# Splitting the hidden-dimension matrix anew in row blocks 0 to 2 of an FNet + GEGLU kernel, and fetching parked sums later

## The chip, the cores and the metric

One core of one Trainium2 chip runs the whole program. The metric is device time in microseconds (us) for one execution. "The profile" is one profiled execution of the kernel before. Its engines are PE (matrix multiply), DVE (vector), ACT (scalar), POOL (GpSimd) and SP (which here only issues transfers).

## What is computed

Four layers alternate on x of 2048 rows by 512 columns, in fp32. Layers 0 and 2 mix tokens by a discrete Fourier transform, layers 1 and 3 are a gated feed-forward block:

```python
a = x @ dft_hid_re.T ; b = x @ dft_hid_im.T          # along the 512 columns
y = dft_seq_re @ a - dft_seq_im @ b                  # along the 2048 rows
x = x + y(layernorm(x))
x = x + (gelu(z @ w_gate) * (z @ w_up)) @ w_down     # z = layernorm(x)
```

## The kernel before, in words

**Precision by three products.** Each fp32 operand is split in two parts: ACT copies a 128x512 tile rounded to fp32r (`hi`, L122), DVE subtracts it from the source (`lo`, L124). `mm3` (L160 to L164) then issues three matmuls: hi by hi (L162), hi or lo by the other's lo or hi (L163, L164). So each tile that PE uses costs one ACT and one DVE instruction first, and each 128x512 tile is 256 KB in a transfer.

**The mixing layers.** `mix` takes the output rows in four row blocks of 512 (b = 0 to 3). For a block the products with the sequence matrices (`ws`) come first, in a Strassen-like form that shares sums of tiles: stage `S2` (`s2(b)`, L820) runs three chains T2, T1 and T3 over k = 0 to 7, staggered; stage `S4` two more. Between and behind them stand the products with the hidden matrices (`wh`, eight tiles (m, c)), in `hid_groups`. In layer 0 the order of stages (`plan`, L400) is FORE, which runs the first products of all four blocks, and then for each block S2, EARLY hid, S4, MID hid, LATE hid. For S2, `make_s2` (L343) forms from tiles of `ws` the sums s1 (L153), s3 and s2 (L150) on DVE, and each is then split.

**Parked sums.** FORE produces for blocks 1 to 3 four 128x512 tiles each (two sums and two "sum" tiles) which POOL writes to DRAM (`put_away`, L247, names `m` and `m_sum`). `fetched` (L252) has SP load them back: at the very head of `s2(b)` (L827 to L829), before any product of that stage. The two `m` tiles are used when chain T2 of the block ends (`based`, L758), the two `m_sum` tiles by the EARLY hid products.

**The hidden matrix.** In layer 0, block 0, each `wh` tile is loaded raw (one 256 KB load), split, used, and both parts are written to DRAM by POOL (`make_hid_first`, L380, with `kept`, L275, whose store is L281). All later blocks, and layer 2, load the two finished parts (two 256 KB loads) and split nothing (`make_hid`, L387).

**What sets the order.** `items` lists all streamed weight tiles. `load_next` (L288) has SP load them some items ahead, `split_next` splits them, `take` hands them to PE. Chores of other layers stand in block 0 too: the split of three down-projection weights, stored by POOL as `wc` (L281, L1010). Results leave through `x_add` (L202), also on POOL. Every engine runs its instructions in program order, and the order itself is made by a scheduler that simulates the program with a few numbers on the machine (`machine_as_traced`, L1396), one of them `DMA_PACKET_NS`. SP's and POOL's transfers are thus each one fixed row of instructions, and a transfer that may not start yet holds up all behind it on that engine.

Of the kernel before, what the change touches and what calls it, by code (L numbers as in the profile page):

```python
# [9 lines left out]
F32 = mybir.dt.float32  # L10
# [7 lines left out]
ND = D // P  # L18
# [25 lines left out]
NEAR_PAIR = 8  # L44
LEAD_PAIR = 4
WHD_AT = 6
GAPS = 1, 2, 1
LEAD = 3
NK = NS // 2
# [1 line left out]
SP_DELAY_NS = 3000  # L51
DEPTH = 1
DMA_BYTES_PER_NS = 21.5
DMA_PACKET_NS = 37


@with_exitstack
def fnet_geglu(ctx: ExitStack, tc: tile.TileContext, x_in, ws, wh, whc, wgu, wdc, out):
# [58 lines left out]
    def f32(ap):  # L117
        return ap.bitcast(F32)
# [133 lines left out]
    def fetched(key):  # L252
        t = sb.get()
        nc.sync.dma_start(t, away.pop(key))
        return t


    whs = {(m, c): dram.tile([P, 1024], F32, name=f"wh{m}_{c}") for m in range(2) for c in range(ND)}
# [13 lines left out]
    def halves(t):  # L272
        return t[:, :512], t[:, 512:]

    def kept(place, parts, by_name=False):  # L275
        for n, t in enumerate(parts):
            to, t = halves(place)[n], f32(t)
            if by_name:
                to = place.rearrange("p (h m c) -> p h m c", h=2, m=2)[:, :, n]
                t = t.rearrange("p (h c) -> p h c", h=2)  # L280
            nc.gpsimd.dma_start(to, t)  # L281


    items, needs, outside = [], {}, set()
# [41 lines left out]
    def plain(v):  # L326
        p = split_slot(v)
        sb.put(v)
        return p

    s1s, s2s, s3s, cs, held = {}, {}, {}, {}, {}
# [4 lines left out]
    def make_a11(k):  # L336

        def run(v):
            held[k] = v
            return split_slot(v)  # L340
        return run

    def make_s2(k, keep):  # L343
        def run(a21, a22, *a11):
            a11 = a11[0] if a11 else held.pop(k)
            s1 = a22
            if keep:
                held["A22", k], s1 = a22, sb.get()
            plus(s1, a21, a22)
            minus(a21, a11, a21)  # L350
            minus(a11, s1, a11)
            s1s[k], s2s[k], s3s[k] = s1, a11, a21
            return split_slot(a11)
        return run
# [4 lines left out]
    def make_s1(k):  # L359
        return lambda: plain(s1s.pop(k))  # L360

    def make_s3(k):
        return lambda: plain(s3s.pop(k))
# [9 lines left out]
    def product_parts(m, c):  # L373

        t = cs.pop((m, c))
        p = split_minus(t) if m else split_slot(t)
        sb.put(t)
        return p

    def make_hid_first(m, c):  # L380
        def run(v):
            w = plain(v)
            kept(whs[m, c], w)
            return product_parts(m, c), w
        return run

# [3 lines left out]
    def skewed(n):  # L390

        skew = SKEW[n - 2]
        return [(i, k - i * skew) for k in range(NK + (n - 1) * skew) for i in range(n) if 0 <= k - i * skew < NK]
# [6 lines left out]
    def plan(layer):  # L400

        fore, steps = FORE[layer], []
        if layer == 0:
            steps += [(None, "FORE")]
        else:
            steps += [(b, "A11") for b in range(fore)] + [(b, "A12") for b in range(fore)]
        for b in range(NB):
            if b >= fore:
                steps += [(b, "A11"), (b, "A12")]
            if b in PAIRED[layer] or b - 1 in PAIRED[layer]:  # L410
                steps += [(b, "S2"), (b, "S4")] + [(b, "PAIR")] * (b - 1 in PAIRED[layer])
            else:
                steps += [(b, "S2"), (b, EARLY_HID), (b, "S4"), (b, MID_HID), (b, LATE_HID)]
        return steps
# [15 lines left out]
    def mix_items(layer):  # L430
        def raw(make, *tiles):
            items.append((F32, tiles, make, None))

        for b, what in plan(layer):
            if what == "FORE":
                for j in range(NS):
                    for c in range(FORE[layer]):
                        raw(plain, ws[c * 2 * NS + j])
                continue
            tiles = [[ws[(b * 2 + m) * NS + k] for k in range(NS)] for m in range(2)]  # L440
            (a11, a12), (a21, a22) = ((r[:NK], r[NK:]) for r in tiles)
            hold = b >= FORE[layer]
            if what == "A11":
                for k in range(NK):
                    raw(make_a11(k) if hold else plain, a11[k])
            elif what == "A12":
                for k in range(NK):
                    raw(plain, a12[k])
            elif what == "S2":
                for i, k in skewed(3):  # L450
                    if i == 0:
                        raw(make_s2(k, b in KEEP22[layer]), a21[k], a22[k], *(() if hold else (a11[k],)))
                    else:
                        raw(make_s1(k) if i == 1 else make_s3(k))
            elif what == "S4":
                for i, k in skewed(2):
                    if i == 0:
                        raw(make_s4(k), a12[k])
                    elif b in KEEP22[layer]:
                        raw(make_a22(k))  # L460
                    else:
                        raw(plain, a22[k])
            elif what == "PAIR":
                for name, k in PAIR_ORDER:
                    items.append((F32R, (piece_of(whd, k, name),), whole, NEAR_PAIR))
            else:
                for m, c in what:
                    if layer == 0 and b == 0:
                        items.append((F32, (wh[m * ND + c],), make_hid_first(m, c), (m, c)))
                    else:  # L470
                        items.append((F32R, halves(whs[m, c]), make_hid(m, c), (m, c)))

# [235 lines left out]
    def mix(layer):  # L708
        hid, sums, chores, hid_left = {}, {}, [], [0]
# [110 lines left out]
        def s2(b):  # L820
            last, fore = b == NB - 1, b < FORE[layer]
            if b == 0:
                lend("z")
                lend("x")
            if fore:
                chains[b] = [ps8.get() for _ in range(2)]
                if b:  # L827
                    sums[b] = [fetched((layer, b, c)) for c in range(2)]
                    cs.update({(0, c): fetched((layer, b, c, "sum")) for c in range(2)})  # L829
            chain, one, three = chains.pop(b), [ps8.get() for _ in range(2)], [ps8.get() for _ in range(2)]  # L830
            sides[b] = one, three
            if last:
                queue.extend([run for fetch in later.pop("fetches") for run in (None, None, None, None, fetch)])
            for i, k in skewed(3):
                if i == 0:
                    six(chain, "T2", k, fore and k == 0, k == NK - 1)
                elif i == 1:
                    six(one, "T1", k, k == 0, k == NK - 1, "T12" if last else None)
                else:
                    six(three, "T3", k, k == 0, k == NK - 1)  # L840
                if k < NK - 1:
                    continue
                if i == 0:
                    us[b] = [based(b, c, p) for c, p in enumerate(chain)]
                    ps8.put(*chain)
                    if fore:
                        sb.put(*sums.pop(b))
                for c in range(2):
                    if i == 1:
                        v = cs[1, 2 + c] = sb.get()  # L850
                        plus(v, us[b][c], one[c])
                    elif i == 2:
                        plus(cs[1, 2 + c], cs[1, 2 + c], three[c])
# [203 lines left out]
    def geglu(w, layer):  # L1057
# [50 lines left out]
        def up(n):  # L1108
            if layer == 1 and w == 0:
# [4 lines left out]
                if n % 2 == 0 and n // 2 + 1 in down_making:  # L1114
                    queue.extend(down_making.pop(n // 2 + 1)[1])
            if layer == w == 1 and 0 <= n - WHD_AT < ND and PAIRED[2]:
                load, runs = weight_steps(n - WHD_AT, whc, whd)
                load()
# [186 lines left out]
        if before_mix:  # L1305
            lend("x")
            lend("z")
            for k in (*range(NT, NK), *range(NT)):
                queue.extend([lambda k=k: second_rows(layer + 1, k), *[None] * GAPS[0]])
            for k in range(NK):  # L1310
                queue.extend([lambda k=k: combine(k), *[None] * GAPS[1]])
            for k in range(NK):
                queue.extend([lambda k=k: combine_late(k), *[None] * GAPS[2]])

# [63 lines left out]
    sums = [run for k in range(NK) for run in (lambda k=k: combine(k), lambda k=k: combine_late(k))]  # L1378
# [17 lines left out]
def machine_as_traced():  # L1396
# [7 lines left out]
    spec.DMA_BUS_BYTES_PER_NS_PER_ENGINE = DMA_BYTES_PER_NS  # L1404
    spec.DMA_MIN_TRANSFER_TIME = DMA_PACKET_NS
    depth = {mybir.EngineType.DVE: DEPTH, mybir.EngineType.Activation: DEPTH}
# [53 lines left out]
```

## Time and profile before

| what | value |
|---|---|
| median of 3 timed runs | 1598.64 us (1596.57, 1598.84, 1598.64) |
| the profiled execution itself | 1597.56 us |
| its span, first to last instruction | 1595.8 us |
| busy: PE, DVE, ACT, POOL | 1585.2, 1236.1, 857.9, 235.9 us |
| granted TensorE clock | 1.000 |

Busy time of PE hides small waits, so PE's rate is the better gauge: how many matmuls start in a stretch of time. In the tables of stretches below, each engine has its busy time and, in brackets, the number of its instructions. "Issue to landing" of a transfer is the time from its issue instruction to its last byte's signal. Queue q1 is SP's, q0 is POOL's.

### The profile page before, as it was taken

To read this page: it belongs to the slowest core of one execution; us is meant where nothing else is said; L and a number is where in the kernel's file an instruction comes from. 1 tells how busy PE (TensorE), PEld (TensorE's weight loads), DVE (VectorE), ACT (ScalarE), POOL (GpSimd) and SP (SyncE) were. 2 spreads that over 40 slices of the span, in tenths; PEclk is the share of its full clock that TensorE was granted. 3 is DMA by queue.
4 is the path that set the end of the run, shared out by engine and by line. 5 is a ranking of instruction groups with operands and counts; after the bars stand their busy time and mean duration, and the time that the engine had idled before them with its cause. 6 is when DMAs were issued, how large, how long until landed. Compare 5 with 4: busy or idle time off the path is not lost.

```text
span 1595.8 us, 23078 instructions
## 1 busy us (share of the span) xinstructions
PE 1585.2 (99%) x7026; PEld 1312.0 (82%) x7026; DVE 1236.1 (77%) x2148; ACT 857.9 (54%) x1680; POOL 235.9 (15%) x410
## 2 busy tenths in 40 slices
PE   9999999999999999999999999999999999999998
PEld 7888788888888888888888888888888888888887
DVE  8999979689789695666869987788985458754475
ACT  7864454545766652756777434446446435433361
POOL 2212300112545201330032000001002000000000
PEclk9999999999999999999999999999999999999999
DMA  9949987787999899996876687768998966896452
GB/s 360 326 167 321 358 279 235 235 292 259 338 341 325 283 346 305 305 323 199 310 231 234 241 269 247 245 236 239 254 375 226 293 204 229 302 280 203 137 190 56
DMA packets 251804, 422.86 MB, mean 265 GB/s; under 512 B 28864, under 2 KB 82112, under 8 KB 250656
## 3 DMA queue, kind: packets, MB, share of 16 engines
q1 hardware_dynamic: 227024, 338.26, 66.0%
q0 software_dynamic: 23840, 82.73, 14.2%
q8 instruction: 56, 0.92, 0.2%
q10 hardware_dynamic: 816, 0.39, 0.1%
q14 instruction: 68, 0.56, 0.1%
HBM read 339.74 MB, written 81.53 MB: 264 GB/s over the span
## 4 chain that ended last, share of the span: by engine, by line
PE 93%; DVE 3%; DMA 2%; issue 1%; ACT 1%; SPq 0%; POOL 0%; DVEq 0%; ACTq 0%; POOLq 0%
PE p L163 31%; PE p L164 31%; PE p L162 31%; DVE s L124 2%; DMA s<-ws 1%; DVE s L150 1%; ACT s L122 0%; DMA xwide<-ws 0%; DVE s L153 0%; DMA wc<-s 0%; DMA xwide<-wh 0%; SPq L298 0%; ACT s L553 0%; DVE st L512 0%; DVE xwide L150 0%
## 5 line engine op out<-in xcount | busy, mean ns | idle before, releaser
L163 PE MATMUL p<-s,s 128*128 128x512 f32 (+1 forms) x2334 | 902.2, 388 | 0.1
L164 PE MATMUL p<-s,s 128*128 128x512 f32 (+1 forms) x2334 | 891.5, 388 | 0.0
L162 PE MATMUL p<-s,s 128*128 128x512 f32 (+1 forms) x2334 | 874.1, 388 | 3.0 <-ACT s L122 2.7
L122 ACT ACTIVATE s<-s 128x512 fp32r<-128x512 f32 (+1 forms) x839 | 471.7, 608 | 341.6 <-DVE s L150 115.1
L124 DVE TENSOR_TENSOR s<-s,s 128x512 fp32r<-128x512 f32 (+1 forms) x839 | 526.5, 661 | 64.9 <-ACT s L122 55.6
L162 PEld LDWEIGHTS p<-s,s 128*128 128x128 f32 x2334 | 438.0, 188 | 95.6 <-ACT s L122 5.1
L163 PEld LDWEIGHTS p<-s,s 128*128 128x128 f32 x2334 | 438.2, 188 | 90.7 <-DVE s L124 0.9
L164 PEld LDWEIGHTS p<-s,s 128*128 128x128 f32 x2334 | 438.2, 188 | 89.8
L153 DVE TENSOR_TENSOR s<-s,p 128x512 f32<-128x512 f32 x291 | 195.4, 682 | 205.1 <-PE p L164 112.2
L150 DVE TENSOR_TENSOR s<-s,s 128x512 f32<-128x512 f32 (+1 forms) x411 | 247.0, 616 | 8.4 <-PE p L163 3.0
L157 ACT ACTIVATE s<-p 128x512 f32<-128x512 f32 x246 | 143.6, 593 | 150.0 <-PE p L164 140.5
L1054 ACT ACTIVATE s<-s 128x512 f32<-128x512 f32 x112 | 70.1, 629 | 119.0 <-DVE s L153 117.0
L281 POOL DMA_DIRECT2D wb<-s x84 | 46.7, 564 | 120.2 <-ACT s L122 89.9
L1068 DVE TENSOR_TENSOR s<-s,s 128x512 f32<-128x512 f32 x84 | 57.8, 688 | 1.8
L153 DVE TENSOR_TENSOR s<-s,s 128x512 f32<-128x512 f32 (+1 forms) x73 | 42.9, 591 | 8.9 <-DMA s<-ws 5.9
L122 ACT ACTIVATE s<-xwide 128x512 fp32r<-128x512 f32 (+1 forms) x61 | 36.8, 616 | 23.8 <-DVE xwide L150 5.1
L553 ACT ACTIVATE s<-s,shift,rstd 128x512 f32<-128x512 f32 x58 | 46.2, 806 | 4.2 <-DVE shift L517 4.1
L526 POOL TENSOR_SCALAR rstd<-rstd 128x1 f32<-128x1 f32 x48 | 15.4, 320 | 222.4 <-ACT junk L525 221.9
L243 POOL DMA_DIRECT2D out<-wide x8 | 5.2, 656 | 271.6 <-DVE wide L153 181.0
L124 DVE TENSOR_TENSOR s<-xwide,s 128x512 fp32r<-128x512 f32 (+1 forms) x61 | 40.5, 674 | 2.3 <-ACT s L122 2.2
L243 POOL DMA_DIRECT2D x<-wide x12 | 7.9, 661 | 219.1 <-DVE wide L153 146.5
L523 ACT ACTIVATE junk<-s 128x512 f32<-128x512 f32 x43 | 26.8, 624 | 22.4 <-DMA s<-x 22.2
(107 smaller groups left out, 520.7 us busy)
## 6 DMA issues: line engine op xcount, KB each, us to landing
s<-ws SPq DMA_DIRECT2D x367, 256.0 KB, 5.1
s<-wb SPq DMA_DIRECT2D x294, 256.0 KB, 5.3
s<-wc SPq DMA_DIRECT2D x196, 256.0 KB, 4.7
wb<-s POOLq DMA_DIRECT2D x98, 256.0 KB, 4.8
s<-wh SPq DMA_DIRECT2D x85, 256.0 KB, 5.2
s<-x SPq DMA_DIRECT2D x55, 256.0 KB, 4.6
xwide<-ws SPq DMA_DIRECT2D x49, 256.0 KB, 4.0
wc<-s POOLq DMA_DIRECT2D x49, 256.0 KB, 6.1
```

The source lines that it names most:

```text
L122: nc.scalar.activation(hi, src, AF.Copy)
L124: nc.vector.tensor_tensor(lo, src, f32(hi), op=ALU.subtract)
L150: nc.vector.tensor_tensor(out, a, b, op=ALU.subtract)
L153: nc.vector.tensor_tensor(out, a, b, op=ALU.add)
L157: nc.scalar.activation(v, src, AF.Copy)
L162: nc.tensor.matmul(ps, ah, bh, start=start, stop=False, skip_group_check=True)
L163: nc.tensor.matmul(ps, ah, bl, start=False, stop=False, skip_group_check=True)
L164: nc.tensor.matmul(ps, al, bh, start=False, stop=stop, skip_group_check=True)
L281: nc.gpsimd.dma_start(to, t)
L553: nc.scalar.activation(z, x, AF.Identity, bias=shift, scale=rstd)
L1054: nc.scalar.activation(t, g, AF.Gelu_apprx_tanh)
L1068: nc.vector.tensor_tensor(t, t, v, op=ALU.mult)
```

## The change

Three things change, all for layer 0, and nothing else in what is computed.

- Blocks 0, 1 and 2 (`KEEP_AT = 2`) load `wh` raw and split it anew. Only block 2 stores the parts. Block 3 and layer 2 load the stored parts as before.
- In blocks 1 to 3 the two `m` loads stand at k = 4 of chain T2 and the two `m_sum` loads at k = 7 (`BACK_AT = 4, 7`). In layer 2 all four stand at k = 0.
- `DMA_PACKET_NS`, a number of the scheduler's machine, is 39 instead of 37.

```diff
+BACK_AT = 4, 7
+KEEP_AT = 2
...
-DMA_PACKET_NS = 37
+DMA_PACKET_NS = 39
...
-    def make_hid_first(m, c):
+    def make_hid_first(m, c, keep):
         def run(v):
             w = plain(v)
-            kept(whs[m, c], w)
+            if keep:
+                kept(whs[m, c], w)
             return product_parts(m, c), w
         return run
...
-                    if layer == 0 and b == 0:
-                        items.append((F32, (wh[m * ND + c],), make_hid_first(m, c), (m, c)))
+                    if layer == 0 and b <= KEEP_AT:
+                        items.append((F32, (wh[m * ND + c],), make_hid_first(m, c, b == KEEP_AT), (m, c)))
...
             if fore:
                 chains[b] = [ps8.get() for _ in range(2)]
-                if b:
-                    sums[b] = [fetched((layer, b, c)) for c in range(2)]
-                    cs.update({(0, c): fetched((layer, b, c, "sum")) for c in range(2)})
...
             for i, k in skewed(3):
+                if b and fore and i == 0 and k == (0 if layer else BACK_AT[0]):
+                    sums[b] = [fetched((layer, b, c)) for c in range(2)]
+                if b and fore and i == 0 and k == (0 if layer else BACK_AT[1]):
+                    cs.update({(0, c): fetched((layer, b, c, "sum")) for c in range(2)})
```

In the changed kernel's rows below, line numbers are two to four higher: L300 is the old L298 (a load of the weight stream), L256 the old L254 (a fetch), L283 the old L281 (a store of parts), L155 and L152 the old L153 and L150.

**SP, head of block 1's S2.** Before, behind block 0's loads of `x`: two `ws` tiles, three parked tiles, then the third tile of the first pair of sums (s_2231), and so on.

```order
L190 DMA s_2199<-x 128x512
L298 DMA s_2233<-ws 128x512
L298 DMA s_2229<-ws 128x512
L254 DMA s_2278<-m_1_0_sum 128x512
L254 DMA s_2274<-m_1_0_1369 128x512
L254 DMA s_2276<-m_1_1_1375 128x512
L298 DMA s_2231<-ws 128x512
L298 DMA s_2308<-ws 128x512
L298 DMA s_2306<-ws 128x512
```

The same place in the changed kernel; s_2215 is the tile that corresponds to s_2231.

```order
L192 DMA s_2183<-x 128x512
L300 DMA s_2213<-ws 128x512
L300 DMA s_2282<-ws 128x512
L300 DMA s_2217<-ws 128x512
L300 DMA s_2323<-ws 128x512
L300 DMA s_2286<-ws 128x512
L300 DMA s_2215<-ws 128x512
L300 DMA s_2284<-ws 128x512
L300 DMA xwide<-wh 128x512
```

The parked tiles are gone from here (the first comes back eight rows below this piece), but other `ws` tiles have moved up, so the tile of the sum is the sixth behind `x` in both.

**DVE, the same place.** Before, the sum that waits for s_2231 follows on one subtraction and two splits.

```order
L150 TENSOR_TENSOR s_2136<-s_2134,s_2136 128x512
L124 TENSOR_TENSOR s_2336<-xwide,s_2335 128x512
L124 TENSOR_TENSOR s_2408<-xwide,s_2407 128x512
L153 TENSOR_TENSOR s_2231<-s_2229,s_2231 128x512
L150 TENSOR_TENSOR s_2229<-s_2233,s_2229 128x512
```

In the changed kernel it follows on five splits, and stands two rows further down in DVE's program; the next sum needs s_2284.

```order
L126 TENSOR_TENSOR s_2292<-s_2120,s_2291 128x512
L126 TENSOR_TENSOR s_2302<-s_2051,s_2301 128x512
L126 TENSOR_TENSOR s_2388<-xwide,s_2387 128x512
L126 TENSOR_TENSOR s_2312<-xwide,s_2311 128x512
L126 TENSOR_TENSOR s_2223<-s_2053,s_2222 128x512
L155 TENSOR_TENSOR s_2215<-s_2213,s_2215 128x512
L152 TENSOR_TENSOR s_2213<-s_2217,s_2213 128x512
L155 TENSOR_TENSOR s_2284<-s_2282,s_2284 128x512
```

**POOL, block 2.** Before, behind the stores of block 1's rows, stands only the store of turned rows (`t`) and the small norm steps (`rstd`).

```order
L206 DMA x_1_90<-s_3009 128x512
L647 DMA t_0_0_2594<-wide 128x2048
L526 TENSOR_SCALAR rstd<-rstd 128x1
L527 TENSOR_TENSOR rstd<-rstd,power 128x1
L526 TENSOR_SCALAR rstd<-rstd 128x1
L527 TENSOR_TENSOR rstd<-rstd,power 128x1
```

In the changed kernel 16 stores of `wh` parts stand here (gone from block 0), twelve of them between and behind the norm steps and right ahead of the stores of `wb`; four more stand ahead of this piece.

```order
L650 DMA t_0_0_2582<-wide 128x2048
L529 TENSOR_SCALAR rstd<-rstd 128x1
L530 TENSOR_TENSOR rstd<-rstd,power 128x1
L283 DMA wh_2_107<-s_3586 128x512
L283 DMA wh_3_108<-s_3608 128x512
L529 TENSOR_SCALAR rstd<-rstd 128x1
L283 DMA wh_2_103<-s_3640 128x512
L530 TENSOR_TENSOR rstd<-rstd,power 128x1
L283 DMA wh_2_107<-s_3587 128x512
```

Up to the first store of `wh` in block 0 all five engines' rows are the same before and after.

## The prediction

> **What bounds the kernel now.** I read the page first, for its span and for what its chain of waits runs through.
>
> ```profile
> span 1595.8 us, 23078 instructions
> PE 1585.2 (99%) x7026; PEld 1312.0 (82%) x7026; DVE 1236.1 (77%) x2148; ACT 857.9 (54%) x1680; POOL 235.9 (15%) x410
> PE 93%; DVE 3%; DMA 2%; issue 1%; ACT 1%; SPq 0%; POOL 0%; DVEq 0%; ACTq 0%; POOLq 0%
> ```
>
> PE is busy for 99% of the span, so only what keeps PE waiting, or stops keeping it waiting, can move the time. The change touches no matmul. Next I asked for the busy time by stretches, chosen along layer 0's blocks, with one stretch of later work as a gauge.
>
> ```profile
> 3.00:25.00 22.00, 20.81 (x95) 16.56 (x94) 19.04 (x44) 16.06 (x29) 3.71 (x5) 1.00 1.04 376
> 400.00:500.00 100.00, 100.00 (x443) 82.81 (x442) 84.18 (x161) 68.37 (x147) 51.70 (x90) 1.00 0.97 333
> ...
> 110.00:150.00 40.00, 40.00 (x178) 33.15 (x177) 37.71 (x67) 19.47 (x34) 7.78 (x13) 1.00 0.77 260
> 150.00:178.00 28.00, 28.00 (x125) 23.12 (x124) 27.50 (x49) 13.58 (x26) 15.47 (x24) 1.00 0.95 350
> 178.00:192.00 14.00, 12.10 (x50) 8.77 (x49) 11.01 (x19) 4.50 (x8) 1.62 (x3) 1.00 1.04 399
> 192.00:242.00 50.00, 50.00 (x223) 41.35 (x222) 41.66 (x69) 28.60 (x61) 3.28 (x8) 1.00 0.84 283
> 242.00:275.00 33.00, 33.00 (x147) 27.35 (x146) 30.84 (x51) 16.72 (x29) 2.79 (x5) 1.00 0.69 223
> 275.00:318.00 43.00, 43.00 (x192) 35.59 (x191) 29.77 (x52) 22.72 (x50) 4.56 (x10) 1.00 0.74 240
> 318.00:346.00 28.00, 28.00 (x125) 23.18 (x124) 24.50 (x42) 10.14 (x19) 5.41 (x10) 1.00 0.92 321
> ```
>
> From 400 to 500 us 443 matmuls start, one every 0.2257 us: that is PE at its full pace. In 178 to 192, the head of block 1's S2, 50 start in 14 us, and 50 x 0.2257 = 11.3, so **2.7 us are lost there**. The opening (3 to 25) loses time too, but the rows of all engines are the same up to 108 us, so that stays. The other stretches run at full pace. The waits of 160 to 200 us and the issues and instructions there tell what the loss comes from.
>
> ```profile
> PE p L162 <- ACT s L122: 1.8, 2, 1.6
> DVE s L153 <- DMA s<-ws: 2.9, 1, 2.9
> 179.82 1.28 DVE L124 TENSOR_TENSOR s<-xwide,s 128x512 fp32r<-128x512 f32 x2
> 184.03 0.69 DVE L153 TENSOR_TENSOR s<-s,s 128x512 f32<-128x512 f32 x1 [2.93 <-DMA s<-ws]
> 163.47 5.00 SPq L190 DMA_DIRECT2D s<-x  x4
> 168.57 1.29 SPq L298 DMA_DIRECT2D s<-ws  x2
> 169.95 1.12 SPq L254 DMA_DIRECT2D s<-m_sum  x1
> 172.43 1.86 SPq L254 DMA_DIRECT2D s<-m  x2
> 174.35 4.05 SPq L298 DMA_DIRECT2D s<-ws  x3
> 174.35 9.66 DMA s<-ws
> ```
>
> The chain: SP issued the tile s_2231 at 174.35, behind three parked tiles; it landed 9.66 us later, at 184.01; DVE, done at 181.10 with what stood ahead, waited 2.93 us for it; behind it, in ACT's order, stood the split that PE needed. PE ran out at 184. Why 9.66 us? The transfers of 168 to 184 us:
>
> ```profile
> DMA packets 2547, 6.28 MB, mean 393 GB/s; under 512 B 384, under 2 KB 384, under 8 KB 2547
> q0 software_dynamic: 1129, 3.71, 60.6%
> q1 hardware_dynamic: 1418, 2.58, 42.7%
> wc<-s POOLq DMA_DIRECT2D x10, 256.0 KB, 7.5
> s<-x SPq DMA_DIRECT2D x1, 256.0 KB, 5.2
> ```
>
> The sixteen engines are full at 393 GB/s, and POOL's stores have the larger part. SP gets 2.58 MB in 16 us, one 256 KB tile every 1.63 us.
>
> **The change part by part.**
>
> *The stores of wh leave block 0.*
>
> ```profile
> L281 POOL DMA_DIRECT2D wh<-s x16: 539/542/555, 108.9 to 157.6; - x16
> 157.56 0.54 POOL L281 DMA_DIRECT2D wh<-s  x1 [2.55 <-DVE s L124]
> 158.15 0.72 POOL L281 DMA_DIRECT2D wc<-s  x1
> 162.97 0.71 POOL L281 DMA_DIRECT2D wc<-s  x1 [2.54 <-DVE s L124]
> ```
>
> The last of the 16 is issued at 157.6, ten us ahead of the jam. The `wc` stores that fill 163 to 176 wait for DVE's splits (2.54 us at 162.97), not for the wh stores, and those splits keep their place in DVE's program. So this removal frees 110 to 160 us, where PE loses nothing. I cost it at 0; at most it lets some `wc` stores go a us or two earlier, which would be a gain of the same order at the jam, and that end I keep in the range.
>
> *The parked tiles leave the head of S2.* Three loads go from ahead of s_2231; the order shows three other `ws` loads in their place, so s_2215 is the sixth tile behind the `x` loads as before. I count with SP's pace: the `x` loads are issued by 168.47 and the last lands 5.2 us later, at 173.7 at the latest; six tiles at 1.63 us make 183.4. The loads before it wait for fewer stores (a fetch waited till 172.43 for a slot), which is worth up to 1 us; I take half: 183.0. DVE has two more rows ahead, at 0.60 us (the 179.82 row has two in 1.28), so it stands ready at 181.10 + 1.2 = 182.3, and waits 0.7 us. The next sum needs the seventh tile, at 184.6, when DVE comes to it at 183.0 + 1.2 = 184.2: 0.4 more. So DVE's wait falls from 2.93 to 1.1 us, by 1.8, and PE's loss from 2.7 to 0.9. I call the **gain 1.8 us**. The bounds: if the tiles come before DVE asks, the gain is the whole 2.7; if SP's place in line is all that counts and the sixth tile lands at 184.01 again, DVE still waits 1.7 + 0.4 us, and 0.8 is gained; and since the rows of block 1 are dealt out anew, below nothing is possible too.
>
> [...]
>
> *The fetches themselves come later.* Four 256 KB loads per block move by three to eighteen places in SP's program. The first use of `m` tiles is where DVE adds them to chain T2:
>
> ```profile
> 207.72 1.28 DVE L153 TENSOR_TENSOR s<-s,p 128x512 f32<-128x512 f32 x2
> ```
>
> Without the loss that is about 205. In the new order the first `m` tile is the nineteenth behind `x`: nine tiles at 1.63 us till 188, when POOL's stores are through, and ten at 0.93 us (256 KB at the 283 GB/s of 192 to 242, where the DMA share is 0.84) make about 197.5. That is 7 us early, so I cost it at 0 us; if that cover were gone, each us of lateness is a us. Layer 2's fetches stay at the head of S2.
>
> *Blocks 1 and 2 split wh.* Eight splits each, on ACT and DVE:
>
> ```profile
> L122 ACT ACTIVATE s<-s 128x512 fp32r<-128x512 f32 (+1 forms) x839 | 471.7, 608 | 341.6 <-DVE s L150 115.1
> 166.54 2.82 DVE L124 TENSOR_TENSOR s<-s,s 128x512 fp32r<-128x512 f32 x5
> ```
>
> Eight at 0.61 us are 4.9 us of ACT; eight at 0.60 (the row of 166.54, less overlap) 4.8 us of DVE, for each block. DVE is idle 8.3 of 50 us in 192 to 242, and 2.2 + 13.2 us in block 2 (242 to 318); ACT has more. So it fits behind PE: 0 us. If the idle time lies in the wrong place, up to 4.8 us of DVE's delay per block, of which block 0 (the same splits, DVE 37.71 of 40 us, PE at full pace) shows none reaching PE. Half as many bytes of wh are loaded in each of the two blocks, 2.1 MB less.
>
> *Block 2 stores wh*: 16 x 256 KB = 4.2 MB, 10.7 us of all engines at 393 GB/s, less 5.3 us for the 2.1 MB not loaded. In 275 to 318 the DMA engines are free for 0.26 x 43 = 11.2 us. It fits, if the stores end by 318: 0 us, with an end of its own on the other side (below).
>
> *The scheduler's 39 for 37* deals out rows of later stages anew up to about 1225 us. No row moves out of need there, and those stretches lose nothing now; any new wait is a loss. 0 us, up to 1.5 (one wait like the longest of PE here, 1.6).
>
> The sum: 1597.56 - 1.8 = **1595.8** for an execution like the profiled one. That one is 1.1 us below the median of the three timed runs and 1.0 above the lowest; the mean of all four is 1597.9, which I take as the kernel's time: 1597.9 - 1.8 = **1596.1**.
>
> **The rivals.**
>
> *The jam stays.* For it: POOL's `wc` stores keep their place, and the tile stays sixth. Against: fewer slot waits, three foreign loads gone. Gain 0 to 0.8: 1597.1 to 1597.9, or some tenths above, with the wait moved to another tile of the same stage.
>
> *The wait goes wholly.* For it: 1 us of earlier issue on each of the loads, and `wc` stores freed of the queue behind wh, would be enough. Against: SP's pace of 1.63 us. Gain 2.7: 1595.2.
>
> *The jam moves to block 3 (slower).* Twelve of the wh stores stand in POOL's program between the norm steps and right ahead of the `wb` stores of 316 us. If the splits that they wait for come only with the last hid products, the stores run past 318 us, into block 3's S2. There the DMA share is 0.92: 0.08 x 28 = 2.2 us are free. Twelve stores take 12 x 0.67 = 8 us; what is beyond 2.2 delays the `ws` loads as at 174 us. It decides when more than 2.2 us' worth, four stores, trail past 318. With all twelve, 5.8 us of delay, less DVE's idle 3.5 us in that stretch: 2.3 us lost for sure, 5.8 at worst. 1596.1 + 2.3 to 5.8 = 1598.4 to 1601.9. Against: block 0 has the same stores spread over 108.9 to 157.6, ahead of its last products.
>
> [...]
>
> **How the numbers follow.** The jam shrinks (forecast) 0.50, at 1595.3 to 1597.0. It goes wholly 0.20, at about 1595.2. It stays 0.17, about 1597.5. It moves to block 3, or a like wait arises in a later stage, 0.13, at 1598 to 1602. Runs scatter by about 1 us to each side. The range 1594.2 to 1599.6 takes in the whole gain on a low run, and the first part of the slower case. A difference of 0.2% (3.2 us) is about what a measurement of this kernel can tell from no change; against the median of 1598.64, faster means below 1595.4. That is most of the second case and a little of the first: 0.24. Slower means above 1601.8: 0.08. Within: 0.68.
>
> **What would show it.** In the changed profile, 178 to 192 us should have some 58 matmuls instead of 50, and DVE's wait for a `ws` tile there should be about 1 us, not 2.9. The waits of 192 to 318 us should hold nothing for PE; POOL's last wh store should be issued ahead of 318. If PE loses time at 318 to 350 behind a split whose `ws` tile landed late, the third rival holds; if the loss stands at 178 to 192 unchanged, the first. Wrong altogether would be a wait in the opening or in layers 1 to 3 above 1.5 us.

## The result, and the profile after

The changed kernel takes **1596.13 us** in the median of 22 runs (1594.59 to 1597.35), the kernel before, run beside it, 1598.41 (22 runs, 1595.25 to 1600.47). The ratio is 0.9986, 95% interval 0.9980 to 0.9993: 2.3 us (1.1 to 3.2) are gained, inside the 0.2% that the prediction called no difference. The forecast was 1596.1. The profiled execution took 1594.87 us.

The page of the changed kernel: its span, the engines' busy time, and the chain that ended last. DVE's share of that chain was 3% and is 0%.

```profile
span 1593.1 us, 23069 instructions
PE 1585.2 (100%) x7026; PEld 1313.6 (82%) x7026; DVE 1245.9 (78%) x2164; ACT 865.0 (54%) x1696; POOL 233.4 (15%) x410
PE 85%; issue 11%; DMA 3%; SPq 0%; POOL 0%; ACT 0%; POOLq 0%; DVE 0%
```

The same stretches as before, for the changed kernel (stretch, its length, busy time and instructions of PE, PEld, DVE, ACT, POOL, then granted clock, DMA share, GB/s):

```profile
150.00:178.00 28.00, 28.00 (x126) 23.17 (x125) 27.24 (x50) 15.00 (x28) 12.77 (x19) 1.00 0.70 251
178.00:192.00 14.00, 14.00 (x62) 11.34 (x61) 13.96 (x25) 5.82 (x10) 1.08 (x2) 1.00 1.04 400
192.00:242.00 50.00, 50.00 (x222) 41.41 (x221) 44.76 (x74) 31.78 (x67) 4.05 (x8) 1.00 0.75 252
242.00:275.00 33.00, 33.00 (x148) 27.31 (x147) 30.94 (x52) 18.29 (x34) 4.40 (x8) 1.00 0.67 220
275.00:318.00 43.00, 43.00 (x191) 35.63 (x190) 34.52 (x61) 24.56 (x53) 14.55 (x26) 1.00 0.83 288
318.00:346.00 28.00, 28.00 (x125) 23.17 (x125) 27.16 (x46) 12.92 (x23) 3.79 (x7) 1.00 0.94 330
```

178 to 192 us has 62 matmuls where it had 50, and PE is busy throughout. Everything that the change put into blocks 1 and 2 (more busy time of DVE and ACT from 192 us on) lies beside a full PE.

To see the loss more sharply than such counts allow, I take the starts of the 741st and the 961st matmul (about 170 to 222 us) and subtract 220 times 0.2267 us, the full pace (the mean step from start to start in 400 to 500 us, in both profiles). This is the **head loss** below: 3.06 us before, 0.22 after. The tables count two matmuls that only reach into the stretch, so 64 in 14 us is the full pace; the prediction's 2.7 us for the same loss was a little small. 2.84 us less here and 0.43 less in the opening, which varies by itself, against 0.46 more later (most of it near 847 us) and 0.1 more behind the last matmul, make the 2.7 between the two profiled executions (1597.56 and 1594.87).

How DVE and SP get there: DVE's rows at the place of the sum that waited 2.93 us, and SP's issues ahead of it.

```profile
180.95 0.68 DVE L126 TENSOR_TENSOR s<-s,s 128x512 fp32r<-128x512 f32 x1
181.55 0.68 DVE L155 TENSOR_TENSOR s<-s,s 128x512 f32<-128x512 f32 x1
```

```profile
161.36 4.25 SPq L192 DMA_DIRECT2D s<-x  x4
165.72 9.06 SPq L300 DMA_DIRECT2D s<-ws  x7
```

The sum (L155 at 181.55) follows on the split ahead of it without a wait. Its tile, still the sixth behind `x`, was issued at 170.93 and had landed at 180.86 (before: 174.35 and 184.01). The first `x` load was issued at 161.36 where it was 163.47, 2.1 us earlier: a wait for a slot that DVE sets free stood before it (1.84 us, at a `ws` load) and stands now at the third `x` load (2.16). What the `x` loads themselves wait for, SP's own queue in 158 to 180 us says, first before, then after:

```profile
SPq L190 <- DMA wc<-s: 2.3, 1, 2.3
```

```profile
SPq L192 <- DVE s L126: 2.2, 1, 2.2
```

Before, the fourth `x` load waited till 168.14 us for a slot that a store of `wc` on POOL's queue set free. After, no `x` load waits for a store; the fourth is issued at 164.88, 3.3 us earlier. It lands 1.7 us earlier, at 171.66 for 173.36.

### The profile page after: what moved, and what is told of

It is laid out like the page before. It is cut to its first block, busy times and chain, and to the rows that moved or that the text cites. A ratio compares the mean times of both kernels' runs of the same rounds, so it can differ in the third digit from the quotient of the medians.

```text
span 1593.1 us, 23069 instructions
## 1 busy us (share of the span) xinstructions
PE 1585.2 (100%) x7026; PEld 1313.6 (82%) x7026; DVE 1245.9 (78%) x2164; ACT 865.0 (54%) x1696; POOL 233.4 (15%) x410
## 4 chain that ended last, share of the span: by engine, by line
PE 85%; issue 11%; DMA 3%; SPq 0%; POOL 0%; ACT 0%; POOLq 0%; DVE 0%
PE p L164 28%; PE p L165 28%; PE p L166 28%; DMA s<-ws 1%; DMA s<-wb 1%; DMA wide<-x 1%; DMA out<-wide 0%; POOL out L245 0%; SPq L300 0%; SPq L232 0%; SPq L192 0%; SPq L1048 0%; ACT s L124 0%; ACT s L556 0%; POOLq L1460 0%
## 5 line engine op out<-in xcount | busy, mean ns | idle before, releaser
L124 ACT ACTIVATE s<-s 128x512 fp32r<-128x512 f32 (+1 forms) x848 | 476.6, 607 | 326.1 <-DVE s L152 112.9
L155 DVE TENSOR_TENSOR s<-s,p 128x512 f32<-128x512 f32 x284 | 190.8, 683 | 195.0 <-PE p L166 111.8
L152 DVE TENSOR_TENSOR s<-s,s 128x512 f32<-128x512 f32 (+1 forms) x411 | 246.9, 617 | 4.8 <-DMA s<-ws 2.5
L283 POOL DMA_DIRECT2D wb<-s x84 | 46.0, 549 | 118.9 <-ACT s L124 81.9
L124 ACT ACTIVATE s<-xwide 128x512 fp32r<-128x512 f32 (+1 forms) x68 | 41.0, 616 | 34.9 <-DVE xwide L155 7.2
L126 DVE TENSOR_TENSOR s<-xwide,s 128x512 fp32r<-128x512 f32 (+1 forms) x68 | 45.2, 676 | 6.9 <-ACT s L124 6.9
L155 DVE TENSOR_TENSOR s<-s,s 128x512 f32<-128x512 f32 (+1 forms) x70 | 41.0, 588 | 4.9 <-DMA s<-ws 3.2
L283 POOL DMA_DIRECT2D wc<-s x42 | 30.3, 723 | 73.3 <-ACT s L124 50.6
```

What stands on the lines that cost most here:

```text
L124: nc.scalar.activation(hi, src, AF.Copy)
L126: nc.vector.tensor_tensor(lo, src, f32(hi), op=ALU.subtract)
L152: nc.vector.tensor_tensor(out, a, b, op=ALU.subtract)
L155: nc.vector.tensor_tensor(out, a, b, op=ALU.add)
```

## Experiments

Three theories. **F**: what counts is what stands ahead of the tile in SP's program; the parked tiles' removal is the gain. **P** (with **S**): POOL's stores make the jam, by slowing SP's loads while both queues have work (P) and by holding slots that the `x` loads need (S). **N**: the scheduler's number did it. The rival to all is scatter: two executions of the same rows differ by some 1 us.

The ratio is taken against the runs of the kernel before that stood beside each; it is not exactly the quotient of the medians. "Other loss" is what PE loses behind the head beyond what the kernel before loses there. Both losses are those of one profiled execution, which can lie off the median: that of the four loads more is the fastest of its ten, that of a third of wc to block 2 the slowest of its eleven.

| kernel | median us | ratio to before | profiled us | head loss us | other loss us |
|---|---|---|---|---|---|
| before | 1597.76 to 1598.41 | 1 | 1597.56 | 3.06 | 0 |
| changed | 1596.13 | 0.9986 (0.9980-0.9993) | 1594.87 | 0.22 | 0.4 (847 us) |
| number 39 alone | 1598.56 | 1.0007 (0.9998-1.0016) | 1598.82 | 4.26 | 0 |
| fetch later alone | 1597.52 | 1.0002 (0.9993-1.0011) | 1596.31 | 1.09 | 0 |
| the same again | 1597.43 | 0.9995 (0.9986-1.0004) | 1597.56 | 2.30 | 0 |
| wh part alone | 1596.97 | 0.9994 (0.9985-1.0003) | 1596.91 | 1.83 | 0 |
| changed, with 37 | 1596.33 | 0.9993 (0.9984-1.0002) | 1596.79 | 1.82 | 0.8 (448 us) |
| wc work to block 1 | 1601.95 | 1.0023 (1.0013-1.0032) | 1601.60 | 0.0 | 6.3 (263 us) |
| four loads more | 1597.59 | 0.9998 (0.9988-1.0008) | 1595.93 | 0.84 | 0.3 |
| four small loads more | 1597.31 | 0.9995 (0.9986-1.0005) | 1596.00 | 0.67 | 0 |
| wc stored twice | 1609.31 | 1.0071 (1.0056-1.0086) | 1609.02 | 13.56 | 0 |
| a third of wc to block 2 | 1599.89 | 1.0005 (0.9996-1.0014) | 1601.19 | 0.0 | 6.7 (335 us) |
| a third of wc to block 3 | 1596.34 | 0.9988 (0.9979-0.9997) | 1595.42 | 0.0 | 0.7 |
| before, two slots more | 1596.24 | 0.9990 (0.9981-0.9999) | 1595.92 | 0.0 | 1.0 (576, 1364 us) |

### The parts of the change, one at a time

Fetch later alone: the kernel before with

```diff
+BACK_AT = 4, 7
+KEEP_AT = 0
```

> The later fetches alone: wh is split once in block 0 and its parts are stored there as before, the scheduler's number is 37. In SP's program the tile that DVE's first sum waits for stands fifth behind the x loads instead of sixth, with no parked tile ahead of it. Theory F (the fetches' place in line made the wait): the tile lands by about 182, DVE waits under 0.7 us at the head of block 1's S2, PE loses under 0.7 us in 178 to 192, and the time is about 2 us below before. Theory S (the wh stores of block 0 made it, by holding up SP's loads ahead): the first x load is still issued at about 163.5, the tile lands at 183 or later, PE loses 1 us or more, and the time falls by 0.8 us or less.

The wh part alone:

```diff
+BACK_AT = 0, 0
+KEEP_AT = 2
```

> The new place of wh alone: blocks 0 to 2 split it anew, block 2 stores it, but the four parked tiles are fetched at the head of S2 as before, and the scheduler's number is 37. The tile that DVE waits for stands seventh behind the x loads, three parked tiles ahead of it. Theory F: the wait is as in before, DVE 2.5 us or more, PE loses about 2.7, the time is within 0.5 us of before. Theory S: the first x load is issued at about 161.4, seven tiles at 1.5 us make 182.5, PE loses 0.8 us at most, and the time is 1.5 to 2.3 us below before.

The number alone, in the kernel before:

```diff
-DMA_PACKET_NS = 37
+DMA_PACKET_NS = 39
```

> Before with the scheduler's number 39 for 37 and nothing else. The rows of all engines are the same up to behind block 2's products. Theories F and S: nothing changes at the head of block 1's S2, PE loses about 2.7 us there, the time is within 0.5 us of before. Theory N (the number did it, by dealing out later rows anew): the time falls by 1 us or more.

The whole change with the old number:

```diff
-DMA_PACKET_NS = 39
+DMA_PACKET_NS = 37
```

> The change with the scheduler's number left at 37. Theories F and S: as the changed kernel, no more than 0.3 us lost at the head of block 1's S2, about 2.3 us below before. Theory N: a good part of the gain is gone, less than 1.3 us below before.

**N falls**: 39 alone leaves the rows of the head as they were, and the head loss is 4.26. The stretch 178 to 192 and DVE's wait in that kernel:

```profile
178.00:192.00 14.00, 10.82 (x46) 7.97 (x44) 9.70 (x16) 4.50 (x8) 1.62 (x3) 1.00 1.03 391
```

```profile
DVE s L153 <- DMA s<-ws: 4.2, 2, 3.4
```

So 3.06 and 4.26 are two samples of one order. The changed kernel with 37 is a second sample of the changed order, since its rows at the head are those of the changed kernel:

```profile
178.00:192.00 14.00, 13.04 (x55) 9.94 (x54) 11.26 (x19) 5.04 (x9) 1.08 (x2) 1.00 1.02 387
```

```profile
DVE s L155 <- DMA s<-ws: 2.7, 2, 2.4
```

DVE's row for the first of the two sums, whose tile is the sixth:

```profile
183.74 0.69 DVE L155 TENSOR_TENSOR s<-s,s 128x512 f32<-128x512 f32 x1 [2.35 <-DMA s<-ws]
```

There the sixth tile landed at 183.72, not 180.86, and the head loss is 1.82, where at most 0.3 was expected. The order before loses 3.1 to 4.3 us, the changed order 0.2 to 1.8. That scatter is as large as any one part's effect, which is why the medians of the parts (none of whose intervals excludes 1) cannot be added up.

The wh part alone got the head loss down to 1.83 with the parked tiles still at the head, which the prediction had costed at 0. Only 0.8 of it lie in 178 to 192; the other 1.0 come at 207.5, where PE waits for a DVE sum while DVE is busy 22.98 of 23 us (192 to 215). Its stretch and its SP waits:

```profile
178.00:192.00 14.00, 13.79 (x60) 10.71 (x59) 13.37 (x23) 5.79 (x11) 2.21 (x4) 1.00 1.04 406
```

```profile
SPq L192 <- DVE s L126: 2.1, 1, 2.1
SPq L256 <- DMA wc<-s: 1.6, 1, 1.6
```

Here too the `x` loads wait for no store (the fourth is issued at 165.54), and it is a fetch of a parked tile that waits for one. But the fourth `x` load lands at 173.52, and the tile of the first sum at 183.78, both as before (173.36 and 184.01). DVE nevertheless waits 0.39 us for that tile and not 2.93: it has five splits to do ahead of the sum where it had two, as in the changed kernel. What this part gains at the head is thus, in this profile, not an earlier tile but DVE's rows dealt out anew.

Fetch later alone gave nothing in the median, so I ran it again.

> The kernel before with only the parked tiles fetched later, once more, since its profile showed a loss of 1.1 us at the head of S2 and its median no gain. Theory F alone: loss about 1 us again, 2 less than before, and a median 1 to 2 us below that of before, in the end. Theory F with S (the wh stores of block 0 leave the fourth x load late, issued at 166.5 to 168, so that the loss varies as before's does): a loss anywhere from 1 to 4 us, and again a median within 0.8 us of before.

In its second profile, its stretch 150 to 178, what PE waits for, and what SP waits for:

```profile
150.00:178.00 28.00, 26.00 (x115) 21.19 (x115) 27.41 (x50) 14.70 (x28) 15.44 (x24) 1.00 0.95 349
```

```profile
PE p L164 <- DVE s L155: 2.0, 1, 2.0
```

```profile
SPq L192 <- DMA wc<-s: 1.3, 1, 1.3
```

The wait for the `ws` tile is nearly gone (the tile stood fifth behind `x` and landed at 182.66, in the first profile at 181.51, with five splits ahead of the sum in both), and in 178 to 192 PE loses nothing in either profile (63 and 64 matmuls). But a new wait has come 7 us earlier, at 175 to 177, for a sum of a DVE busy 27.4 of 28 us; the first profile has it at the same place, at 174.6 to 175.7. So the jam was not the only thing close to the edge: moving the fetches deals DVE's rows out anew, and without the wh part this place loses 1 to 2 us. Why PE comes to wait for that sum there, no run isolates. The fourth `x` load waits for a `wc` store in all four profiles of orders that store both wh and wc in block 0 with 93 slots (issued at 166.5 to 168.1), and in none of the six that take the wh stores out and leave wc whole (164.4 to 165.5). **S holds**, as to the issue. By the landing less is left: that load landed at 173.4 to 173.7 us in the four, and at 171.7 to 174.5 in the six.

### Is it POOL's stores?

The kernel before with the splits and stores of wc moved to block 1:

```diff
-BEFORE = {0: (0, 1, 2)}
+BEFORE = {1: (0, 1, 2)}
```

> The kernel before with the splits of wdc (and their 20 stores to wc) moved from block 0 to block 1; the parked tiles stay at the head of block 1's S2, ahead of the ws tiles. Theory P (POOL's stores make the jam: sixteen DMA engines shared by two queues): between 163 and 184 us SP has the engines for itself, a 256 KB tile goes in 0.65 to 1.0 us instead of 1.63, the ws tiles behind the parked ones land before DVE asks, and the matmuls 740 to 960 lose under 0.5 us (before: 3.1). Time then 1598.0 - 3 = 1595.0 to 1596, if block 1, which gets the splits of wdc in DVE's and ACT's program, loses nothing; a loss of block 1 after 195 us is counted apart. Theory F (only what stands ahead in SP's program counts): the parked tiles still stand there, the loss stays at 2 us or more, time 1597 to 1598.5.

The changed kernel with each store of a split `wc` part issued twice, the second to a place that nobody reads:

```diff
                     kept(to, t, place is not wblocks)
+                    if place is wdd and n < 3:
+                        for h in range(2):
+                            nc.gpsimd.dma_start(dram.tile([P, 512], F32, name=f"again{n}_{i}_{h}"), f32(t[h]))
```

> The changed kernel in which POOL stores each divided part of wc twice in block 0, the second time into a place that nobody reads: twice the suspected competitor. Theory P with shares by backlog (the deeper queue gets more): SP's pace goes from 1.55 to some 2.2 us a tile, the sixth tile behind x lands 3 to 4 us later, and matmuls 740 to 960 lose 3 to 5 us; time 1598.5 to 1600. Theory P with equal turns between the two queues: while POOL has stores to do SP's pace stays at 1.5 to 1.7 us, the tile lands where it did, the loss at the head of S2 stays 0.2 to 1.8, and the time is 1596 to 1597 (the stores only run on some 6 us longer, to about 190). Theory F (POOL's stores don't matter): no difference at all in the landings of 163 to 190 us.

Without POOL's `wc` stores there is no jam. This run alone doesn't settle it, since SP's rows come out otherwise too: its parked tiles have all landed by 165.14 us. The stretch, and the two queues in 174 to 192 us (packets, MB, share of 16 engines):

```profile
178.00:192.00 14.00, 14.00 (x64) 11.58 (x63) 11.45 (x19) 6.48 (x12) 0.00 (x0) 1.00 0.78 280
```

```profile
q1 hardware_dynamic: 2304, 4.20, 67.3%
q0 software_dynamic: 242, 0.79, 13.1%
```

With twice the stores, the queues in 175 to 199 us:

```profile
q0 software_dynamic: 1803, 5.87, 60.7%
q1 hardware_dynamic: 2186, 3.98, 43.1%
```

The time from one landing of an SP tile to the next tells more than the shares. I read it from the transfers in each trace:

```
before, 173.4 to 184.0:           1.67 1.80 1.76 1.78 1.76 1.88     then from 188.5 on 0.67 to 0.68
changed, 175.7 to 185.9:          1.63 1.77 1.75 1.52 1.76 1.73     then from 187.2 on 0.65 to 0.69
changed with 37, 172.9 to 185.5:  1.86 1.84 1.76 1.77 1.75 1.89 1.77
wc stored twice, 172.7 to 199.4:  1.72 to 1.86, fifteen in a row
wc work to block 1, 181.8 to 187.9: 0.63 to 0.68
```

Two steady paces stand out: about 1.77 us a tile of 256 KB while POOL's stores move, 0.67 when it has none. Twice the stores leave the pace where it is, they only make it last longer (to 199 us). Whether a deeper queue would get more, this does not test: POOL has 7 to 8 stores issued and not landed at 172 to 180 us in this kernel, and 6 to 8 before and after the change. The packets of the two queues differ in number and size in 175 to 199 us: 2186 of q1 with 3.98 MB / 2186 = 1.8 KB each, 1803 of q0 with 5.87 / 1803 = 3.3 KB, so SP has 40% of the bytes. How the engines choose between the two queues, no run shows.

Gaps in POOL's traffic are one source of the scatter in these profiles. In the changed kernel's profile, tiles landed at 172.29 and 173.40, 0.63 and 1.11 after the one ahead: POOL's packets took only 14% of the engines at 171.0 to 171.5 us (58% with 37), although six of its stores were issued and had not landed. Why they paused, no run shows. In the same rows with 37 the two tiles took 1.86 and 1.84, the fourth `x` load landed 1.2 us later (172.85), and the sixth tile came 2.9 us later. P holds as to the pace. The times that it was to give were all missed (at most 1600 expected, 1609.31 measured): the price of wc twice (13.6 us) is more than the slower landings. Its two waits:

```profile
PE p L164 <- ACT s L124: 5.7, 1, 5.7
PE p L165 <- DVE s L126: 4.1, 2, 3.2
```

The doubled stores keep their slots and parts longer, so SP issues nothing between 173.3 and 178.4 us, and the `wh` tile issued at 178.89 then takes 9.73 us more. Here the chain of that kernel passes from a store to DVE, to SP, to the tile ("..." leaves out pieces):

```profile
164.74 8.72 DMA wc<-s
...
173.48 0.70 DVE s L126
...
178.40 0.33 SPq L300
...
178.89 9.73 DMA s<-wh
```

The work that was moved to block 1 did not fit there: 6.3 us are lost at 263 us. That is the price of theory P's cure, not of the jam.

### What does a place in SP's line cost?

The changed kernel with four loads that nobody uses, at the head of block 1's S2, of 256 KB and of 16 KB:

```diff
+            if layer == 0 and b == 1:
+                extra = [sb.get() for _ in range(4)]
+                for n, t in enumerate(extra):
+                    nc.sync.dma_start(t[:, :512], ws[n][:, :512])      # 32 for 512 in the other kernel
+                sb.put(*extra)
```

> The changed kernel with four more loads of 256 KB (rows of ws that nobody uses) at the head of block 1's S2, on SP's queue: the suspected cost put back by itself, without parked tiles or stores to wait for. Three of them come to stand ahead of the tile s_2215. Theory F: each costs its transfer at SP's pace, 1.5 to 1.6 us; s_2215 lands some 3 to 4.6 us later after its place's predecessors than in the run with the small loads, and the matmuls 740 to 960 lose 3 to 5 us; time 1598 to 1600. Rival (the parked tiles cost because they waited for their slots or their stores, not because of their bytes): these loads wait for nothing, the loss stays as in the changed kernel, 0.2 to 1.8 us, time 1596.1.

> The same four loads at the same places in SP's program, but with 16 KB each (32 of 512 columns). Theory F, by bytes: they cost next to nothing, the loss of matmuls 740 to 960 is 0 to 1.5 us and the time 1596 (three ws tiles of the changed kernel even stand behind them now). If a load's place counts by its packets or by its issue (128 rows each, as the large ones), the loss is that of the large loads, 3 to 5 us, time 1598 to 1600.

The stretch with the large loads, then with the small ones:

```profile
178.00:192.00 14.00, 13.47 (x60) 10.83 (x59) 12.26 (x21) 5.41 (x10) 1.08 (x2) 1.00 1.04 403
```

```profile
178.00:192.00 14.00, 13.62 (x61) 10.95 (x60) 13.96 (x24) 6.40 (x11) 1.53 (x3) 1.00 1.05 402
```

F's expectation for the large loads missed (3 to 5 us of head loss, 0.84 measured), and that for the small ones came true in the head loss (0.67). SP's rows are the same, three of the extra loads ahead of s_2215. From the `ws` tile ahead of them to the last of the three took 2.7 us with the large ones (0.79, 0.65, 1.28) and 2.8 with the small ones (1.39, 0.19, 1.24). That is no fair comparison of the sizes, since a pause of POOL's packets helped the large loads (39% of the engines at 175.5 to 177 us); at the steady pace three large ones would take 5.3, by my estimate (3 x 1.77). The two `ws` tiles behind took 3.5 and 2.5 us, and s_2215 landed at 181.93 and 180.51. A place in line was thus not a fixed 1.6 us in these runs: it was 0.7 to 1.8 as POOL's packets happened to move at that moment, and three loads of a sixteenth of the bytes cost far more than a sixteenth (2.8 us against the estimated 5.3). The medians (1597.59 and 1597.31, 1.2 to 1.5 us above the changed kernel's, with overlapping intervals) do not separate the sizes, and both lie between the two times that were expected in each case (1596, or 1598 to 1600); the median executions may have lost more than the profiled ones.

The other way round, **the place without the change**: the kernel before with 95 slots.

```diff
-NSLOT = 93
+NSLOT = 95
```

> The kernel before with 95 slots for 93. In its order three ws tiles stand ahead of the parked tiles, right behind the x loads, while the wh stores stay in block 0 and the parked tiles at the head of S2: the theory of the place in line without the change. Theory F: the tile that DVE waited for now stands third, lands at some 173 + 3 x 1.78 = 178.4 us, the wait for it goes; the next ones stand behind the three parked tiles, so some wait of 0 to 2 us may come at 184 to 188. Loss of matmuls 740 to 960: 0 to 2 us (before 3.1 and 4.3), time 1595.5 to 1597.5. Theory S (slots held by stores make the x loads late): with two slots more the fourth x load is issued at 164 to 165.5 rather than 166.5 to 168. If neither holds, loss 3 to 4 us and 1598.

SP's issues, the stretch 178 to 192, and DVE's wait in it:

```profile
161.47 1.30 SPq L190 DMA_DIRECT2D s<-x  x3
163.55 3.65 SPq L298 DMA_DIRECT2D s<-ws  x3
167.29 0.79 SPq L254 DMA_DIRECT2D s<-m  x1
```

```profile
178.00:192.00 14.00, 14.00 (x64) 11.58 (x63) 10.92 (x18) 7.20 (x13) 0.17 (x1) 1.00 1.05 400
```

```profile
DVE s L153 <- DMA s<-ws: 2.1, 1, 2.1
```

The head loss is gone with the wh stores and the parked tiles in place and POOL's stores still moving (in 174 to 184 us q0 moved 2.26 MB and q1 1.80; before, 2.45 and 1.57): the scheduler put the three `ws` tiles of the first sums ahead of the parked ones, and the last `x` load is issued at 162.40. F and S together, then, and once more with DVE's rows dealt out anew. DVE still waits 2.1 us for a tile, at 183.7 to 185.8, and PE doesn't feel it: the next sums come early enough. By these runs two slots are worth as much as the whole change (1596.24 against 1596.13; ratios 0.9990 and 0.9986).

### A version beyond both?

The changed kernel with a third of wc's work in block 2, or in block 3:

```diff
-BEFORE = {0: (0, 1, 2)}
+BEFORE = {0: (0, 1), 2: (2,)}      # 3 for 2 in the other kernel
```

> The changed kernel with the third of wc's three blocks (7 of 20 stores, its loads and splits) moved from block 0 to block 2, where wh is stored as well. Theory P (POOL's backlog of stores makes the pace of 1.78 us a tile on SP's queue): the stores of wc end ahead of the x loads' landing or soon after, SP's tiles land at 0.7 to 1.3 us, DVE waits for no ws tile, and matmuls 740 to 960 lose nothing (changed kernel: 0.2 and 1.8 in two executions). Block 2 gets seven splits and four sums more, some 7 us of DVE where 10.7 us were idle in 242 to 318: if they fit, the time is 1595 to 1595.8; if they don't, as block 1 showed when it got all of wc's work (6.3 us lost), 1 to 3 us are lost there and the time is 1596.5 to 1598.5. Theory L (the loss varies by itself): no difference in the S2 head's loss from the changed kernel's 0.2 to 1.8.

> The same with the third of wc's work in block 3, the last of the stage. Theory P: the S2 head of block 1 loses nothing, as in the run with block 2. Block 3 had 0.8 us of DVE idle in 318 to 346 and 6.9 in 346 to 394: the seven splits and four sums (7 us) do not fit into the first and just into the second; expected loss 0 to 3 us, time 1595 to 1598.

The head loss is nothing in both, as P expects. With block 3 it costs 0.7 us elsewhere, and the time is that of the changed kernel, not better (0.9988 against 0.9986). With block 2 the wait moves to 332 us (6.7 us lost in the profile, the slowest execution of its eleven; median 2.1 us above before, while the ratio's interval holds 1). Its stretch 336 to 344, PE's wait, and the chain there:

```profile
336.00:344.00 8.00, 8.00 (x24) 6.31 (x24) 7.91 (x14) 4.21 (x8) 0.58 (x1) 0.63 1.05 383
```

```profile
PE p L165 <- DVE s L126: 3.5, 1, 3.5
```

```profile
322.82 6.99 DMA wb<-s
...
330.04 0.70 DVE wide L647
```

## Why the prediction was right, step by step

**The bound and the place** held: the gain came from the head of block 1's S2, with no other place as large. The loss there was 3.06, not 2.7. That the forecast of 1596.1 meets 1596.13 so closely is luck: it took the kernel before for 1597.9 where 1598.41 was measured, and the gain for 1.8 where it was 2.3.

**The parked tiles leave the head** (gain 1.8, with 0.8 to 2.7 as bounds). The forecast had the tile land at 183.0; it landed at 180.86 and 183.72 in two executions, on both sides. Its sum had two errors that offset each other: SP's pace behind the `x` loads was taken as 1.63 us a tile, a mean over 16 us, where the steady pace is 1.77, and the last `x` load as landed at 173.7, where it was 171.66 and 172.85. The wait of DVE was put at 1.1 us; it was 0 and 2.7. So the first execution is the second rival, the wait that goes wholly, and the other lies between the forecast and the first rival. The head loss was put at 0.9; it was 0.22 and 1.82, mean 1.0, against a mean of 3.7 for the order before. So 2.6 are gained at the head and 0.4 to 0.8 lost again later: the size is right on the mean, and the single number hid that the place varies by 1.6 us from one execution to the next. Of the mechanism one piece is larger than the forecast made it. With 37 the sum began at 183.74, only 0.3 us earlier than before, and in the wh part alone at 183.80; yet 178 to 192 had 55 and 60 matmuls, not 50. DVE had done more ahead of that sum (five splits for two), work that it would else have done behind it. The forecast counted these rows only as a delay of DVE. No run changes DVE's order alone, so how much of the gain is the earlier tile and how much this order stays open.

**The wh stores leave block 0, at 0**, was the step that failed. It looked for the stores' effect on POOL's queue, where they are indeed done ten us ahead, and missed what the change does to the slots: with the `wh` stores in block 0 the fourth `x` load waited 2.3 us for a slot that a `wc` store held, without them no `x` load waits for a store. It missed DVE's new order too, which in the wh part alone made the difference, as the tile landed no earlier there. That part alone brought the head loss to 1.83, the fetches' move alone to 1.09 and 2.30, each with a new wait of about 1 to 2 us at another place; neither gained what the medians can tell, and together they lose 0.22 and 1.82. The failure did not spoil the sum because the step on the parked tiles took the whole gain for itself.

**POOL's `wc` stores keep their place**, on which the first rival rests: they do, and SP's pace beside them is about 1.77 us a tile, with twice as many too (1.72 to 1.86). The rival's conclusion, that the wait would stay as it was, holds for neither execution, though the one with 37 came near (the tile at 183.72, a DVE wait of 2.7, a loss of 1.8). POOL's stores set the pace, but not when the tiles start (the last `x` load landed 1.7 and 0.5 us earlier than before), nor what DVE does meanwhile.

**Fetches later, 0**: the four parked tiles of block 1 were issued at 185.4 to 189.3 us and landed by 194.7, before the 197.5 that was estimated and ten us before their use; no engine waits for them. **Blocks 1 and 2 split wh, 0**: the table above, PE full from 192 to 318. In the wh part alone block 1 does lose 0.9 us behind a full DVE, at 207.5. **Block 2 stores wh, 0**: POOL's last one stands at 305.98, ahead of the first store of `wb`.

```profile
305.98 0.54 POOL L283 DMA_DIRECT2D wh<-s  x1 [5.19 <-DVE s L126]
307.35 0.54 POOL L283 DMA_DIRECT2D wb<-s  x1 [0.83 <-ACT s L124]
```

So the slower rival, stores that run past 318 us, did not come. It was near: seven more stores in block 2 brought it about, in block 3's S2. The chain ran otherwise than named, not through `ws` loads but through a `wb` store behind the stored parts (6.99 us from issue to landing, DVE's L647 behind it), and the price was 6.7 us in that slowest execution, above the 2.3 to 5.8 of the rival, and 3.8 by the medians, inside them.

**The scheduler's number, 0 to 1.5 later**: 0.4 us at 847 and 0.8 at 448 us in two profiles of the changed order. Whether 39 or 37 is better there is not resolved (0.9986 and 0.9993, overlapping).

## What to carry to other kernels

Where two queues share the DMA engines, find the stretch in which both have work and count tiles at that pace (about 1.77 us a tile here, 0.67 without POOL's stores); here twice the competitor's stores lengthened the stretch (to 199 us) and did not change the pace (1.72 to 1.86). A store cost more here than its queue's time: it also held a slot, for which the fourth `x` load waited 2.3 us. So ask which load waits for the tile that the store still reads, and look at the waits of SP's own queue for it. PE lost less here where DVE had more rows ahead of the same wait (1.83 us with five splits, the tile landing at 183.78, for 3.06 with two, at 184.01), so compare each engine's order in both kernels too. When a loss of 3 us scatters by 1.2 to 1.6 from one execution to the next, one profile of each order is not enough, and the same rows under another name are a cheap second sample.

## What the runs showed of the hardware that was not expected

**Three long waits of PE cost twice.** In three kernels PE waited 3.7 us or more at one place (from one matmul's start to the next), and the matmuls behind started every 0.427 us instead of 0.227 for a while. After 3.7 us (a third of wc to block 2) the granted clock was halved for 6.8 us, after 4.0 (wc work to block 1) for 3.4, and after 5.8 with another 3.6 behind (wc stored twice) for 10.2. The first and the last of these lengths are two and three times the second. Of the 6.7 us lost in the first kernel, 3.0 are the slow matmuls. The stretch 263 to 267 of the kernel with wc's work in block 1, right behind its wait, and 192 to 200 of the one with wc stored twice:

```profile
263.00:267.00 4.00, 3.79 (x10) 3.01 (x11) 3.93 (x8) 2.96 (x6) 0.00 (x0) 0.57 0.98 283
```

```profile
192.00:200.00 8.00, 4.78 (x12) 3.28 (x12) 3.85 (x6) 0.63 (x1) 0.10 (x1) 0.50 1.04 408
```

A wait of 2.2 us (fetch later alone, again) left the clock at 1.00. Why the clock was halved for 6.8 us after the wait of 3.7 and for only 3.4 after that of 4.0, no run isolates. In the traces the halved clock began 0.67 us before PE went on in the first (335.04, 335.71) and 0.10 before in the second (263.11, 263.21).

**The opening varies by itself.** The full clock began at 4.2 to 7.4 us after the first instruction in these profiles (4.23 before, 7.27 in the changed kernel), and the opening's loss ran from 2.3 to 3.3 us, with the same rows in the first 24 us.
